# Attention and two gated blocks on one core: no weight conversions in the attention but one block's, DVE adds the 1e-9, the first products of two chunks interleaved, gates ahead of folds

## The chip, the cores and the metric

The kernel runs on one core of one Trainium2 chip. The metric is the device time of one execution in microseconds (us). The kernel before took 961.48 us, the median of three runs (959.97 to 962.03).

## What is computed

An attention with a bias from positions, then two feed-forward blocks, all in float32 (the weights come as 64-bit words that the kernel converts).

```python
scores = q @ k.T / sqrt(64) + bias        # 4 batches, 8 heads, 576 positions, 64 wide
attn = exp(scores - max); attn = attn / (sum(attn) + 1e-09)
x = attn @ v                              # as 2304 tokens x 512
a = x @ w1; b = x @ w2                    # 512 -> 1024
x2 = (a * b @ w3) @ w_out                 # 1024 -> 1024 -> 512
h = x2 @ w_in; solu = h * softmax(h); out = layernorm(solu) * g @ w_out2
```

## The kernel before

Five engines work from in-order queues of their own: TensorE (PE; PEld is its weight load), VectorE (DVE), ScalarE (ACT), GpSimd (POOL) and SyncE (SP), which issues nearly all DMAs. The order of each queue is the order in which the Python code emits instructions; nothing reorders them later. A float32 product is made of three fp32r matmuls (`three`, L79 to L81): high by high, high by low, low by high. A tile is split into a high half by an ACT cast and a low half by a subtraction on DVE or POOL.

**Bias** (up to 74 us) is not touched.

**Attention** (class `Attention`) goes through 16 pairs of heads in slots, `slot(s)`, ten to a pair. A slot emits, in this order: on ACT an addition of 1e-9 to the sums of exponentials of three slots ago (`inverse(0, ...)`, L410), the high halves of transposed blocks (L505), the copy of a finished output out of PSUM (L507) and one exponential (L403); on DVE the bias addition with row maximum (L396), the reciprocal of those sums (L412) and low halves (L519); on POOL the scaling of the exponentials by the reciprocal (L416); on PE a score product (L383, L79 to L81), four transposes (L426) and four value matmuls (L469). Every 13th slot `conv_ab` starts a conversion of half a block of w1 or w2 from 64-bit words: SP loads 256 KB (tile `wraw`), and from the seventh slot on each slot has one step of it, an ACT step (L69) and four DVE steps (L70 to L73, tile `wx`), and then a store of 128 KB to the tile `big`. There are twelve such halves, for the blocks 1 to 3; `first_ab` of this class converts block 0 in the first slots (tile `wab`).

**Gated** (class `Gated`) computes x2. Tokens come in six chunks `c` of 384, the 1024 columns in eight blocks `f`. `stage1(c, f)`, the *first product*, makes the a and b of a chunk and a block in 24 matmuls in one of two PSUM buffers (tile `ab`); `gate` multiplies them (ACT copy L805, DVE product L806) into the tile `a`, which `put_outs` stores to DRAM (`g_d`). The weights of block f (tile `ab0` to `ab7`) are made by conversions that `convert(n)` emits n steps at a time from a queue: a load of 512 KB (tile `raw`), an ACT step (L69), four DVE steps (L70 to L73, tile `cm`), a high half (ACT, L675) and a low half (DVE, L678). `fold(m)` multiplies w3 and w_out into block m of one matrix (24 matmuls of tile `big` by `w`); `folded` evicts it (ACT L733, DVE L734). `stage2`, the *second product*, takes a stored g (`load_g`, split by `split_g` on ACT and POOL, L61 and L62) by a folded block. The chunk's input x is loaded, summed on POOL (L758) and split (ACT L765, POOL or DVE L767).

The first four first products are emitted in the last slots of the attention (`early`, table `EARLY`), the rest in `run`, one per step: `now` is the step's first product, chunk by chunk; folds stand in steps 17 to 24, second products from step 19 on. A gate is emitted at the start of the step after its product. The conversions of the blocks 4 to 7, of w_out and of w3 are in the queue.

**Solu**, the last block (from 732 us), is not touched.

Of the kernel before, what the change touches and what calls it, by code (L numbers as in the profile page):

```python
# [213 lines left out]
class Attention:  # L214
# [10 lines left out]
    def __init__(self, ch, i, bias, x_d, ga):  # L225
        self.ch, self.nc, self.i = ch, ch.nc, i
        self.bias, self.x_d, self.ga = bias, x_d, ga
        self.pairs = [(p, b) for p in range(NPH) for b in range(NB)]
        self.left, self.right, self.top, self.psl, self.psr = (contextlib.ExitStack() for _ in range(5))
        self.W = {}  # L230
        self.BT = {}
        self.SQ = {}
        self.EV, self.OUT = [], []
        self.later = {}
        self.conv, self.fill = [], []
# [7 lines left out]
    def open_right(self):  # L243
        ch = self.ch
        self.ep = ch.pool(self.right, "ae", "right")
        self.idt = self.ep.tile([128, 128], F, name="idt", tag="idt")
        ch.load(self.idt, self.i["ident"])
        self.eps = self.ep.tile([128, 8], F, name="eps", tag="eps")
        ch.nc.gpsimd.memset(self.eps, 1e-9)
        self.eps = self.eps[:, 0:1]  # L250
        self.tp = ch.pool(self.top, "at", "right")
        self.sps = ch.pool(self.psl, "asp", bufs=2, space=PSUM)
        self.tps = ch.pool(self.psr, "atp", "right", bufs=2, space=PSUM)
        self.ops = ch.pool(self.psr, "aop", "right", bufs=1, space=PSUM)
# [103 lines left out]
    def conv_ab(self, u):  # L358

        ch = self.ch  # L360
        n, hf = divmod(u, 2)
        raw = self.qk.tile([128, 512], U, tag="wraw", name="wraw")
        x = self.qk.tile([128, 256], F, tag="wx", name="wx")
        ch.load(raw.rearrange("p (k f) -> p k f", k=2), self.words(n, 2 * hf, 2))
        nop = lambda: None
        out = lambda: ch.load(self.ga.first[:, n, hf * 256 : hf * 256 + 256].bitcast(F), x)
        return [nop] * 7 + ch.f64_steps(raw.rearrange("p (n t) -> p n t", t=2), x) + [out]

# [36 lines left out]
    def inverse(self, step, n, k, ps, e, st):  # L405
        if k % 2 == 0 and k < 8:
            return
        c = 1 + k % 2
        if step == 0:
            self.nc.scalar.activation(st[:, 4 : 4 + c], st[:, 2 : 2 + c], AF.Identity, bias=self.eps, scale=1.0)  # L410
        else:
            self.nc.vector.reciprocal(st[:, 6 : 6 + c], st[:, 4 : 4 + c])  # L412
# [84 lines left out]
    def slot(self, s):  # L497
# [3 lines left out]
        if s - 3 in SQ:  # L501
            self.inverse(0, *SQ[s - 3])
# [9 lines left out]
        if s - 3 in SQ:  # L512
            self.inverse(1, *SQ[s - 3])
            if SQ[s - 3][1] % 2:
                self.normalise(*SQ[s - 4])
            if SQ[s - 3][1] % 2 or SQ[s - 3][1] == 8:
                self.normalise(*SQ[s - 3])
# [15 lines left out]
        if n < NP:  # L533
# [13 lines left out]
            if s % 13 == 0 and s < 156:  # L547
                self.conv = self.conv_ab(4 + s // 13)
            if self.conv:
                self.conv.pop(0)()  # L550
# [6 lines left out]
class Gated:  # L557
# [8 lines left out]
    EARLY = {7: 0, 10: 1, 12: 2, 14: 3}  # L566
    MID = 8
    FIRST = 4
# [23 lines left out]
    def open_mid(self):  # L592
        ch = self.ch
        self.gp = ch.pool(self.left, "gg")
        gb = ch.pool(self.left, "gb")
        for f in range(1, self.FIRST):
            self.place[f] = gb

    def open_right(self):
# [3 lines left out]
        for f in range(self.FIRST, 8):  # L603
            self.place[f] = self.wp
# [126 lines left out]
    def folded(self, m, ps):  # L731
        t = self.WF[m] = self.wp.tile([128, 2, 512], R, name="wf%d" % m, tag="wf%d" % m)
        self.nc.scalar.copy(t[:, 0], ps)  # L733
        self.nc.vector.tensor_tensor(out=t[:, 1], in0=ps, in1=t[:, 0].bitcast(F), op=ALU.subtract)  # L734

# [77 lines left out]
    def split_g(self, c, f):  # L813
        hi, lo = self.G[(c, f)]
        self.ch.split(hi, lo, lo.bitcast(F))
# [95 lines left out]
    def early(self, n):  # L911

        if n == 0:
            self.queue += [(self.cv_ab, f, w) for f in range(self.FIRST, 8) for w in range(2)]
# [9 lines left out]
        for k in {1: (0,), 2: (1,), 8: (2, 3), 10: (4, 5), 12: (6, 7)}.get(n, ()):  # L924
            self.rests.append(self.first_ab(k))
        if n > 2:
            self.convert(2)
# [4 lines left out]
        if n in self.EARLY:  # L932
            self.stage1(0, self.EARLY[n])
            self.next_x(1, self.EARLY[n])
# [5 lines left out]
    def run(self):  # L940
        steps = [(c, f) for c in range(NC) for f in range(8)]
        late = [(self.cv_win, u) for u in range(8)] + [(self.cv_wo2, f) for f in range(8)]
        late += [(self.mean_rows,)] + [(self.out_wo2, f) for f in range(8)]
        self.last = True
        plan, n = {}, 0
        for s in range(2 * len(steps)):
            many = 0 if s < self.LAG else 1 if s < self.LAG + 8 else 2
            plan[s] = steps[n : min(n + many, max(0, s - self.NEAR))]
            n += len(plan[s])
        for s in range(len(self.EARLY), len(steps) + self.NEAR + 1):  # L950
            m = s - self.FLAG
            fold = 0 <= m < 8
            now = steps[s] if s < len(steps) else None
# [8 lines left out]
            for g in plan[s + 1]:  # L962
                self.load_g(*g)
# [4 lines left out]
            self.convert(6 if fold else 2 if plan[s] else 5)  # L968
            if fold:
                self.folded(m, ps)  # L970
# [5 lines left out]
            if now:  # L976
                self.next_x(now[0] + 1, now[1])
# [242 lines left out]
```

## Time and profile before

| | |
|---|---|
| median of three runs | 961.48 us |
| the profiled execution | 955.43 us, of which the span from first to last instruction 953.6 |
| PE busy | 881.3 us (92%) |
| DVE busy | 627.2 us (66%) |
| ACT busy | 498.7 us (52%) |
| POOL busy | 413.3 us (43%) |
| mean granted clock of TensorE | 0.986 |

Busy shares are means over stages that differ much, so the rows below go by stage. Times in the rows are us from the start of the span; a wait is put down to the engine or DMA that ended last. [...]

### The profile page before, as it was taken

Reading aid. Unit: us, or ns where it says so; the run is one execution under the profiler, and the core shown is the slowest. Engines: PE = TensorE matmul, PEld = TensorE weight load, DVE = VectorE, ACT = ScalarE, POOL = GpSimd, SP = SyncE. Lnnn points to the kernel's source line nnn. Section 1 sums busy time; section 2 is a strip of 40 time slices with the busy share of each in tenths; the row PEclk is TensorE's granted clock in tenths of the full one; section 3 lists DMA queues with packets and bytes.
Section 4 is the critical chain, followed back from the end, with each engine's and each line's share of the span. In section 5 each row is a group of like instructions: output and inputs, shape, how many; then the busy total and the mean of one; then the engine's idle time right before and its main releaser. Section 6 shows DMA issues by size and latency. Waiting matters only on the chain.

```text
span 953.6 us, 16700 instructions
## 1 busy us (share of the span) xinstructions
PE 881.3 (92%) x5890; PEld 791.0 (83%) x5890; DVE 627.2 (66%) x1296; ACT 498.7 (52%) x1086; POOL 413.3 (43%) x465
## 2 busy tenths in 40 slices
PE   5776999999989989899899999988999999999998
PEld 4435889998978978898789999988999888888886
DVE  7999999998989987667565286472511644444442
ACT  8995999999989974334332134222322322233222
POOL 3238788887877650111112175495632222022000
PEclk9998999999999999999999999998999999999999
DMA  4897999999899666474451575575333101101000
GB/s 137 251 305 228 220 260 279 221 308 256 226 257 246 148 213 201 138 219 151 138 171 34 163 231 157 187 238 163 106 124 110 45 23 56 55 23 56 23 23 34
DMA packets 96900, 153.18 MB, mean 161 GB/s; under 512 B 16432, under 2 KB 61360, under 8 KB 96816
## 3 DMA queue, kind: packets, MB, share of 16 engines
q1 hardware_dynamic: 96672, 151.81, 53.9%
q8 instruction: 47, 0.77, 0.3%
q14 instruction: 37, 0.30, 0.1%
q10 hardware_dynamic: 144, 0.29, 0.1%
HBM read 81.40 MB, written 41.30 MB: 129 GB/s over the span
## 4 chain that ended last, share of the span: by engine, by line
PE 61%; DMA 9%; DVE 9%; ACT 9%; issue 6%; POOL 4%; SPq 2%; POOLq 0%; ACTq 0%; DVEq 0%
PE ab L81 10%; PE ab L79 10%; PE ab L80 10%; PE o L81 4%; PE o L80 4%; PE o L79 4%; PE x L80 3%; PE x L81 3%; PE op L469 3%; PE x L79 3%; ACT e L403 3%; DMA k<-kr 3%; PE sp L383 3%; ACT eth L505 3%; PE tp L426 2%
## 5 line engine op out<-in xcount | busy, mean ns | idle before, releaser
L79 PE MATMUL ab<-xh,ab 128*128 128x384 f32 x384 | 130.8, 341 | 9.6 <-ACT ab L675 4.5
L81 PE MATMUL ab<-xh,ab 128*128 128x384 f32 x384 | 130.5, 340 | 1.2 <-DVE ab L678 1.2
L80 PE MATMUL ab<-xl,ab 128*128 128x384 f32 x384 | 130.1, 339 | 0.4 <-DVE xl L767 0.4
L416 POOL TENSOR_SCALAR e<-e,st 128x576 f32<-128x576 f32 x128 | 97.1, 768 | 40.2 <-DVE st L412 39.2
L62 POOL TENSOR_TENSOR gl<-gl,gh 128x384 fp32r<-128x384 f32 x48 | 55.4, 1168 | 132.1 <-ACT gh L61 129.8
L519 DVE TENSOR_TENSOR etl<-tp,eth 128x512 fp32r<-128x512 f32 (+1 forms) x160 | 99.5, 630 | 15.8 <-ACT eth L505 12.3
L383 PE MATMUL sp<-k,q 128*128 128x288 f32 x512 | 92.0, 302 | 11.7 <-DVE st L396 3.9
L403 ACT ACTIVATE e<-e,st 128x576 f32<-128x576 f32 x128 | 100.1, 782 | 3.3 <-DVE st L396 3.2
L396 DVE CUSTOM_DVE_ANT_0 e<-sp,bt 128x576 f32<-128x576 f32 x128 | 95.4, 746 | 2.1 <-PE sp L383 1.7
L426 PE MATMUL tp<-idt,e 128*128 128x128 f32 x576 | 89.0, 276 | 8.0 <-DVE etl L519 4.8
L505 ACT CAST eth<-tp 128x512 fp32r<-128x512 f32 (+1 forms) x160 | 84.5, 539 | 16.5 <-PE tp L426 14.4
L383 PEld LDWEIGHTS sp<-k,q 128*128 128x128 f32 x512 | 75.4, 191 | 16.3 <-DVE st L396 6.4
L1029 DVE TENSOR_REDUCE st<-ab 128x1 f32<-128x1024 f32 x18 | 22.0, 1224 | 99.7 <-PE ab L81 99.7
L1049 POOL TENSOR_TENSOR st<-st,half 128x1 f32<-128x1 f32 x18 | 9.9, 549 | 176.2 <-DVE st L1048 176.2
L79 PEld LDWEIGHTS ab<-xh,ab 128*128 128x128 f32 x384 | 73.2, 191 | 11.9 <-ACT ab L675 5.1
L426 PEld LDWEIGHTS tp<-idt,e 128*128 128x128 f32 x576 | 69.2, 141 | 13.4 <-DVE etl L519 3.9
L81 PEld LDWEIGHTS ab<-xh,ab 128*128 128x128 f32 x384 | 73.2, 191 | 1.8 <-DVE ab L678 1.8
L80 PEld LDWEIGHTS ab<-xl,ab 128*128 128x128 f32 x384 | 73.0, 190 | 0.7 <-DVE xl L767 0.7
L80 PE MATMUL x<-gl,wf 128*128 128x384 f32 x192 | 66.6, 347 | 5.9 <-POOL gl L62 5.9
L469 PE MATMUL op<-eth,v 128*128 128x288 f32 x256 | 65.8, 338 | 6.1 <-ACT o L507 6.1
L192 PE MATMUL ps<-mk,cb 128*32 128x264 bf16 (+17 forms) x1056 | 51.4, 331 | 20.8 <-DVE mk L171 10.5
L79 PE MATMUL x<-gh,wf 128*128 128x384 f32 x192 | 65.8, 343 | 1.8 <-ACT gh L61 1.8
(167 smaller groups left out, 2229.3 us busy)
## 6 DMA issues: line engine op xcount, KB each, us to landing
bias_d<-rs SPq DMA_DIRECT2D x36, 295.5 KB, 3.9
qkr<-in_qk SPq DMA_DIRECT2D x16, 608.0 KB, 5.6
k<-kr SPq DMA_DIRECT2D x32, 288.0 KB, 6.4
x_d<-o SPq DMA_DIRECT2D x64, 144.0 KB, 3.9
g_d<-a SPq DMA_DIRECT2D x48, 192.0 KB, 4.0
gl<-g_d SPq DMA_DIRECT2D x48, 192.0 KB, 2.7
k<-kr SPq DMA_DIRECT2D x32, 256.0 KB, 6.7
raw<-in_wo SPq DMA_DIRECT2D x16, 512.0 KB, 4.0
```

Source lines behind the costliest of these rows:

```text
L62: (eng or self.nc.gpsimd).tensor_tensor(out=lo, in0=x, in1=hi.bitcast(F), op=ALU.subtract)
L79: mm(out, a[0], b[0], start=first, stop=False)
L80: mm(out, a[0], b[1], start=False, stop=False)
L81: mm(out, a[1], b[0], start=False, stop=last)
L383: nc.tensor.matmul(ps[:, half, :HS], w["q"][:, h, q * 128 : q * 128 + 128], w["k"][:, h, x, half * HS : half * HS + HS], start=x == 0, sto ...
L396: self.nc.vector.tensor_tensor_reduce(out=halves(e), in0=ps[:, :, :HS], in1=halves(self.BT[(self.pairs[n][0], k)]), scale=-0.125, scalar=3e38,
L403: self.nc.scalar.activation(e, e, AF.Exp, bias=st[:, c : c + 1], scale=-1.0, accum_out=st[:, 2 + c : 3 + c])
L416: self.nc.gpsimd.tensor_scalar(out=e, in0=e, scalar1=st[:, c : c + 1], scalar2=1.0, op0=ALU.mult, op1=ALU.mult)
L426: tr = lambda c, src: nc.tensor.transpose(ps[: src.shape[1], c * 128 : c * 128 + 128], src, self.idt)
L469: nc.tensor.matmul(w["op"][:, half, :HS], lhs, rhs, start=c == 0 and x == 0, stop=c == 4 and x == 1)
L505: self.nc.scalar.copy(hi, src)
L519: self.nc.vector.tensor_tensor(out=lo, in0=src, in1=hi.bitcast(F), op=ALU.subtract)
```

## The change

The additions of 1e-9 move from ACT to DVE, ahead of the reciprocal, with no `eps` tile. `conv_ab` is gone; all blocks but 0 are converted in the queue of Gated, as whole blocks of 512 columns. Of the first products that stand in the attention's last slots one less is emitted by step count (three, of which the last is of chunk 1); in `run` the chunks 0 and 1 go side by side, block by block. Chunk 1's x is loaded early, into tiles that the folded blocks 4 to 7 use later. In a step with a fold, the step's own gate is emitted ahead of the fold's eviction. Odd blocks of g get their low half on DVE. The loads of g go ahead by up to four. `convert` takes more steps where there is no fold.

```diff
 class Attention
-        self.eps = self.ep.tile([128, 8], F, name="eps", tag="eps")
-        ch.nc.gpsimd.memset(self.eps, 1e-9)
-    def conv_ab(self, u):
...
-    def inverse(self, step, n, k, ps, e, st):
+    def inverse(self, n, k, ps, e, st):
         if k % 2 == 0 and k < 8:
             return
         c = 1 + k % 2
-        if step == 0:
-            self.nc.scalar.activation(st[:, 4 : 4 + c], st[:, 2 : 2 + c], AF.Identity, bias=self.eps, scale=1.0)
-        else:
-            self.nc.vector.reciprocal(st[:, 6 : 6 + c], st[:, 4 : 4 + c])
+        self.nc.vector.tensor_scalar(out=st[:, 4 : 4 + c], in0=st[:, 2 : 2 + c], scalar1=1e-9, scalar2=None, op0=ALU.add)
+        self.nc.vector.reciprocal(st[:, 6 : 6 + c], st[:, 4 : 4 + c])
...
-        if s - 3 in SQ:
-            self.inverse(0, *SQ[s - 3])
...
-            if s % 13 == 0 and s < 156:
-                self.conv = self.conv_ab(4 + s // 13)
-            if self.conv:
-                self.conv.pop(0)()
 class Gated
-    EARLY = {7: 0, 10: 1, 12: 2, 14: 3}
+    EARLY = {7: (0, 0), 10: (0, 1), 14: (1, 0)}
     MID = 8
-    FIRST = 4
...
+    def wf(self, m):
+        return self.place[1 if m > 3 else 2].tile([128, 2, 512], R, name="wf%d" % m, tag="wf%d" % m)
...
-        self.ch.split(hi, lo, lo.bitcast(F))
+        self.ch.split(hi, lo, lo.bitcast(F), self.nc.vector if f % 2 else None)
...
-            self.queue += [(self.cv_ab, f, w) for f in range(self.FIRST, 8) for w in range(2)]
+            self.queue += [(self.cv_ab, f, w) for f in range(1, 8) for w in range(2)]
...
-        for k in {1: (0,), 2: (1,), 8: (2, 3), 10: (4, 5), 12: (6, 7)}.get(n, ()):
-            self.rests.append(self.first_ab(k))
+        if 0 < n < 3:
+            self.rests.append(self.first_ab(n - 1))
+        if n == self.MID:
+
+            for k in range(4):
+                t = self.wf(4 + k)
+                self.X[(1, k)] = [t[:, y, :TC] for y in range(2)]
+                self.load_x(1, k, self.X[(1, k)])
+        for k in {10: (0, 1), 12: (2, 3)}.get(n, ()):
+            self.XS[(1, k)] = self.sum_x(1, self.X[(1, k)], self.xp, "xs", 2)
+        for k in {11: (0, 1), 13: (2, 3)}.get(n, ()):
+            self.split_x(1, k, self.XS.pop((1, k)))
         if n > 2:
-            self.convert(2)
+            self.convert(2 if n < 9 else 3)
...
-            self.stage1(0, self.EARLY[n])
-            self.next_x(1, self.EARLY[n])
+            self.stage1(*self.EARLY[n])
...
+        order = sorted(steps, key=lambda g: g if g[0] > 1 else (0, g[1] // 2 if g[1] < 2 else g[1], g))
+        at = {g: s for s, g in enumerate(order)}
...
-            plan[s] = steps[n : min(n + many, max(0, s - self.NEAR))]
+            plan[s] = [g for g in steps[n : n + many] if at[g] < s - self.NEAR]
...
-            now = steps[s] if s < len(steps) else None
+            now = order[s] if s < len(steps) else None
...
-            for g in plan[s + 1]:
-                self.load_g(*g)
+            while loaded < min(used + 4, len(steps)) and at[steps[loaded]] < s - 1:
+                self.load_g(*steps[loaded])
+                loaded += 1
+            used += len(plan[s])
...
-            self.convert(6 if fold else 2 if plan[s] else 5)
+            self.convert(6 if fold else 2 if plan[s] else 7)
             if fold:
+                if now:
+                    self.gate(*now)
                 self.folded(m, ps)
                 self.convert(6)
...
-            if now:
-                self.next_x(now[0] + 1, now[1])
+            if now and s > 7:
+                self.next_x(max(2, now[0] + 1), s % 8)
```

How this moves instructions, at three places. First DVE's queue in the middle of the attention, in two slots of a pair, before (`etl` is a transposed block's low half, `e` the scores with bias, `st` the sums, `wx` the conversion's tile):

```order
L519 TENSOR_TENSOR etl<-tp,eth 128x512
L70 TENSOR_SCALAR wx<-wx 128x256
L396 ISA e,st<-sp,bt 128x576
L396 ISA st 128x1
L412 RECIPROCAL st<-st 128x2
L519 TENSOR_TENSOR etl<-tp,eth 128x512
L71 TENSOR_SCALAR wx<-wx 128x256
```

and in the change:

```order
L501 TENSOR_TENSOR etl<-tp,eth 128x512
L382 ISA e,st<-sp,bt 128x576
L382 ISA st 128x1
L395 TENSOR_SCALAR st<-st 128x2
L396 RECIPROCAL st<-st 128x2
```

The conversion's steps are gone, and the addition L395 stands directly ahead of the reciprocal that needs it.

Second, PE's queue from the second first product on: the first matmul of each of six consecutive first products (the 23 that follow each are left out). The first number is the PSUM tile's, `xh` is chunk 0's input, `wf4` chunk 1's, and `ab1` to `ab6` are the weights of the blocks. Before:

```order
L79 MATMUL ab_6105<-xh_5891,ab1_6075 128x384
L79 MATMUL ab_6146<-xh_5891,ab2_6096 128x384
L79 MATMUL ab_6193<-xh_5891,ab3_6141 128x384
L79 MATMUL ab_6249<-xh_5891,ab4_6238 128x384
L79 MATMUL ab_6298<-xh_5891,ab5_6247 128x384
L79 MATMUL ab_6343<-xh_5891,ab6_6283 128x384
```

and in the change:

```order
L79 MATMUL ab_6016<-xh_5781,ab1_5985 128x384
L79 MATMUL ab_6081<-wf4_5965,ab0_5813 128x384
L79 MATMUL ab_6121<-wf4_5965,ab1_5985 128x384
L79 MATMUL ab_6173<-xh_5781,ab2_6152 128x384
L79 MATMUL ab_6220<-wf4_5965,ab2_6152 128x384
L79 MATMUL ab_6265<-xh_5781,ab3_6161 128x384
```

PE's products stand at the same places of its queue, but of another chunk and block: chunk 1 comes at the third product, and a new block is needed at every second one.

Third, DVE's queue around the second fold (`wf_6977` and `wf_6930` are the second fold's low halves, `a` a gate, `w` the low half of w3). Before:

```order
L71 TENSOR_SCALAR cm<-cm 128x512 x2
L72 SCALAR_TENSOR_TENSOR cm<-raw,cm 128x512 x2
L73 SCALAR_TENSOR_TENSOR cm<-raw,cm 128x512 x2
L734 TENSOR_TENSOR wf_6977<-ab,wf_6977 128x512
L678 TENSOR_TENSOR w_6973<-cm,w_6973 128x512
L70 TENSOR_SCALAR cm<-cm 128x512
L678 TENSOR_TENSOR w_6975<-cm,w_6975 128x512
L70 TENSOR_SCALAR cm<-cm 128x512
L71 TENSOR_SCALAR cm<-cm 128x512 x2
L72 SCALAR_TENSOR_TENSOR cm<-raw,cm 128x512 x2
L806 TENSOR_TENSOR a<-ab,a 128x384
```

and in the change:

```order
L653 TENSOR_TENSOR w_6917<-cm,w_6917 128x512
L653 TENSOR_TENSOR w_6919<-cm,w_6919 128x512
L70 TENSOR_SCALAR cm<-cm 128x512 x2
L71 TENSOR_SCALAR cm<-cm 128x512 x2
L784 TENSOR_TENSOR a<-ab,a 128x384
L709 TENSOR_TENSOR wf_6930<-ab,wf_6930 128x512
```

The gate stood behind the fold's low half and a run of conversion steps; now it stands directly ahead of the fold's low half. ACT's two copies that feed them move in the same way.

## Rows read from the trace of the kernel before

**Rows 1.** By stage: stretch, length, busy PE PEld DVE ACT POOL, clock, DMA, GB/s.

```profile
78.00:336.00 258.00, 238.04 (x1800) 226.01 (x1799) 236.99 (x609) 232.96 (x596) 206.05 (x232) 0.99 0.91 242
336.00:372.00 36.00, 29.94 (x180) 28.06 (x180) 28.58 (x52) 21.27 (x46) 13.48 (x14) 0.95 0.66 208
372.00:441.00 69.00, 62.91 (x337) 61.31 (x338) 48.19 (x93) 28.04 (x53) 11.24 (x10) 0.95 0.60 180
441.00:500.00 59.00, 53.19 (x256) 46.54 (x255) 35.60 (x60) 18.13 (x33) 8.40 (x7) 0.97 0.46 150
500.00:732.00 232.00, 224.35 (x1238) 218.20 (x1238) 106.78 (x134) 66.67 (x140) 114.81 (x100) 0.99 0.47 148
```

**Rows 2.** Waits of PE from 78 to 335 us: total us, times, longest.

```profile
PE op L469 <- ACT o L507: 5.4, 10, 0.8
PE sp L383 <- DVE st L396: 3.5, 5, 1.6
PE sp L383 <- DMA k<-kr: 3.4, 3, 1.5
PE tp L426 <- DVE etl L519: 2.9, 4, 1.9
PE sp L383 <- DVE wx L72: 2.2, 1, 2.2
```

**Rows 3.** Groups of instructions: busy us, mean ns, idle before.

```profile
L410 ACT ACTIVATE st<-st,eps 128x2 f32<-128x2 f32 (+1 forms) x80 | 23.6, 295 | 2.4
...
L412 DVE RECIPROCAL st<-st 128x2 f32<-128x2 f32 (+1 forms) x80 | 12.6, 157 | 3.0 <-ACT st L410 2.8
...
L70 DVE TENSOR_SCALAR wx<-wx 128x256 f32<-128x256 f32 x12 | 8.5, 712 | 0.0
```

**Rows 4.** The tile wx alone, 78 to 336 us: busy DVE, ACT, clock, DMA.

```profile
78.00:336.00 258.00, 29.76 (x48) 5.20 (x12) 0.99 0.91 242
```

**Rows 5.** Timeline around a conversion step: start us, duration us, engine, line.

```profile
108.30 0.75 POOL L416 TENSOR_SCALAR e<-e,st 128x576 f32<-128x576 f32 x1
...
109.01 1.56 POOL L57 TENSOR_TENSOR ql<-qkr,qh 128x640 fp32r<-128x640 f32 x1
...
109.11 1.60 DVE L70 TENSOR_SCALAR wx<-wx 128x256 f32<-128x256 f32 x1
```

**Rows 6.** Waits of POOL, whole span: total us, times, longest.

```profile
POOL e L416 <- DVE st L412: 39.2, 46, 3.6
```

**Rows 7.** Groups of DVE from 372 to 441 us.

```profile
L73 DVE SCALAR_TENSOR_TENSOR cm<-raw,cm 128x512 uint32<-128x512 uint32 x16 | 10.8, 683 | 0.0
...
L70 DVE TENSOR_SCALAR cm<-cm 128x512 f32<-128x512 f32 x14 | 6.7, 476 | 0.0
```

**Rows 8.** Waits of PE from 335 to 740 us.

```profile
PE x L80 <- POOL gl L62: 5.9, 6, 1.7
PE ab L79 <- ACT ab L675: 4.5, 2, 2.9
PE ab L79 <- DVE a L806: 3.8, 2, 2.2
PE ab L79 <- DVE wf L734: 3.6, 3, 1.4
...
PE x L79 <- ACT gh L61: 1.8, 1, 1.8
```

**Rows 9.** Timeline of SP's queue.

```profile
354.49 0.99 SPq L47 DMA_DIRECT2D raw<-in_w  x2
```

**Rows 10.** Instructions on the tile xl from 330 to 480 us: ns least/median/most, then landing.

```profile
L47 SPq DMA_DIRECT2D xl<-x_d x18: 319/430/694, 336.2 to 455.3; - x18
L758 POOL TENSOR_TENSOR xs<-xh,xl x14: 992/1040/1500, 343.7 to 463.0; 128x384 f32<-128x384 f32 x14
...
DMA to landing us min/median/max: 2.1/4.7/7.5
```

**Rows 11.** Timeline of ACT: the gate's copy after the second first product.

```profile
362.22 0.48 ACT L805 COPY a<-ab 128x384 f32<-128x384 f32 x1 [1.39 <-PE ab L81]
```

More of the change, by code (lines that the diff above doesn't have):

```diff
@@ L234, in __init__ @@
         self.later = {}
-        self.conv, self.fill = [], []
+        self.fill = []
     def open_left(self):
@@ L247, in open_right @@
         ch.load(self.idt, self.i["ident"])
-        self.eps = self.ep.tile([128, 8], F, name="eps", tag="eps")
-        ch.nc.gpsimd.memset(self.eps, 1e-9)
-        self.eps = self.eps[:, 0:1]
         self.tp = ch.pool(self.top, "at", "right")
@@ L356, in load_bias @@
             self.bias.read(t[:, :, :64], row, 2 * p + 1, 512)
-    def conv_ab(self, u):
[L360 to L367, printed above, removed]
     def scores(self, n, k):
@@ L512, in slot @@
         if s - 3 in SQ:
-            self.inverse(1, *SQ[s - 3])
+            self.inverse(*SQ[s - 3])
             if SQ[s - 3][1] % 2:
@@ L594, in open_mid @@
         self.gp = ch.pool(self.left, "gg")
-        gb = ch.pool(self.left, "gb")
-        for f in range(1, self.FIRST):
-            self.place[f] = gb
+        self.place[1] = ch.pool(self.left, "gb")
     def open_right(self):
@@ L602, in open_right @@
         self.wp = ch.pool(self.right, "gw", "right")
-        for f in range(self.FIRST, 8):
+        for f in range(2, 8):
             self.place[f] = self.wp
@@ L731, in folded @@
     def folded(self, m, ps):
-        t = self.WF[m] = self.wp.tile([128, 2, 512], R, name="wf%d" % m, tag="wf%d" % m)
+        t = self.WF[m] = self.wf(m)
         self.nc.scalar.copy(t[:, 0], ps)
         self.nc.vector.tensor_tensor(out=t[:, 1], in0=ps, in1=t[:, 0].bitcast(F), op=ALU.subtract)
+    def wf(self, m):
+        return self.place[1 if m > 3 else 2].tile([128, 2, 512], R, name="wf%d" % m, tag="wf%d" % m)
     def spot(self):
@@ L944, in run @@
         self.last = True
-        plan, n = {}, 0
+        plan, n, loaded, used = {}, 0, 0, 0
         for s in range(2 * len(steps)):
             many = 0 if s < self.LAG else 1 if s < self.LAG + 8 else 2
-            plan[s] = steps[n : min(n + many, max(0, s - self.NEAR))]
+            plan[s] = [g for g in steps[n : n + many] if at[g] < s - self.NEAR]
             n += len(plan[s])
```

## The prediction

> **What bounds the kernel now.** I read the busy time stage by stage first [rows 1]. From 78 to 336 us, the attention, TensorE (PE), DVE and ACT are busy 238, 237 and 233 of 258 us, and the 16 DMA engines 91%. No engine bounds that stage alone; three in-order queues at some 91% hold each other up, and PE stands idle for 20 us. From 336 us on, PE is the engine that all others serve: the tail of the attention (336 to 372) has 6.1 us of PE idle, the first products (372 to 441) 6.1, the folds (441 to 500) 5.8, the second products (500 to 732) 7.7. [...] After 732 us nothing is touched. [...]
>
> Which waits make up the 20 us is in [rows 2]: 5.4 us for ACT's copy of an output out of PSUM, 3.5 for the bias addition on DVE, 3.4 for the keys' DMA, 2.9 for the low half of a transposed block, 2.2 for a conversion step on DVE. The first four end at the engine that is late in that slot, so what makes ACT and DVE late is what counts.
>
> **The attention.** Removed from ACT are 80 additions of 1e-9, 23.6 us [rows 3], and 12 first conversion steps, 5.2 us [rows 4]: 28.8 of 233 us. Removed from DVE are 48 conversion steps, 29.8 us [rows 4]. Twelve loads of 256 KB, twelve stores of 128 KB and their places in SP's queue go too. Added to DVE are 80 additions on 128x2 or 128x1 elements. The trace has none of just this form beside a busy POOL. From below, the nearest row is the reciprocal of the same operand, 157 ns [rows 3]: 12.6 us. From above, the nearest is the conversion step L70, a scalar operation on an SBUF tile as well, at 712 ns [rows 3]: 57 us. That one is long because it ends only with a POOL operation that began before it: the step at 109.11 takes 1.60 us beside a POOL operation from 109.01 for 1.56 [rows 5]. The addition stands directly ahead of its reciprocal, and POOL was idle, waiting for that reciprocal, in 46 of 80 cases at least [rows 6]; there nothing can hold it. In the other 34, half of a usual POOL operation (0.75 us [rows 5]) is 0.38 us: 13 us together. I take 12.6 + 13 = 25.5 us, since the reciprocal is the nearer row: the same operand, the same place. DVE then still has 4 us less, ACT 29 us less. [...]
>
> Of PE's waits I let go: all 2.2 for the conversion step, half of the 5.4 and of the 3.5 (the slots where ACT copies an output also held an addition of 1e-9), two thirds of the 2.9 (ACT there stood for a conversion's DMA), a third of the 3.4: 2.2 + 2.7 + 1.8 + 1.9 + 1.1 = 9.7; less 0.7 for the additions. **Attention: -9 us.** Bounds: -15 if nearly all waits go, -4 if only those go that name a conversion.
>
> **The tail and the first products.** The twelve half conversions come back as six whole ones behind the attention, ahead of the first fold. DVE gets 6 x (2 x 0.48 + 3 x 0.68) = 18 us [rows 7] (the step L71 is taken like L70, the step L72 and the low half like L73), less six low halves at 0.68 that it had there already: +14. Its idle time from 336 to 441 is 36.0 - 28.6 + 69.0 - 48.2 = 28 us [rows 1], so the work fits, if it fits in order: with two chunks side by side a block of weights is wanted every second product, not at each. That removes the waits for a fresh block, 4.5 us, and the shorter of the two waits for a gate, 3.8 - 2.2 = 1.6 us [rows 8]; with them go 3 of the 3.4 us of half clock: -9. But the third product now needs chunk 1 early. Its 16 loads stand behind two loads of raw weights that SP issued from 354.49 for 0.99 us [rows 9], and take SP 0.43 us each [rows 10] and a little between them: SP is done at about 363. Such loads landed 2.1 to 7.5 us after their issue, in the middle 4.7 [rows 10]; these are half as large, so I let the last data be there 3 us later, and two sums and two splits on POOL at about 1.04 us [rows 10] follow: about 370.5. PE is ready for that product at 362.2, where the second one ends [rows 11]; its 24 matmuls at 62.9 / 337 = 0.19 us [rows 1] would end at 366.7. Waiting for its last quarter, it ends at about 371.5: +5 us, and +1.5 for the half clock behind the gap. **Tail and first products: -2.5 us.** Bounds: -10 without the new stall, +5 with it and half of the old waits.
>
> **The folds.** The gate of the product ahead of each fold now stands ahead of the fold's own eviction on ACT and DVE, so the next product's PSUM is free when the fold ends. PE's waits for the fold's low half, 3.6 us, and the 2.2 us wait for a gate, the longer of two, which stands ahead of the third fold [rows 8], have no reason left, and most of the 1.8 us of half clock goes: 7.6, of which I take 6 since the fold's eviction then ends 0.5 us (one gate) later. **Folds: -6 us**, bounds -7.5 and -2.
>
> **The second products.** Half of the 48 low halves of g go from POOL to DVE. PE waits 5.9 us for them on POOL and 1.8 for the high half [rows 8]; the first of each pair stays on POOL, but POOL's queue is shorter, so I let half of these 7.7 us go, less 0.4 for DVE being held by POOL. The earlier loads of g cost nothing: POOL and ACT wait for them behind PE. **Second products: -3.5 us**, bounds -7 and 0.
>
> **The sum** is -9 - 2.5 - 6 - 3.5 = -21. The profiled execution took 955.4 us (span 953.6), so that one would be 934.4; it lay 6.1 us under the median of the three runs, 961.5, which is what is measured: 940.5.
>
> **The rivals.**
> 1. The transfers bound the attention. For: 91% DMA busy at 242 GB/s [rows 1], and PE waits for the keys. Against: 4.6 MB of some 62 leave. Then the attention gains only 4, the second products nothing: -4 - 2.5 - 6 = -12.5, 949.
> 2. DVE becomes the bound before the first fold. For: +14 us of work into 28 us of idle time, of which most stands ahead of gates and may not be usable. Then the 14 come through to PE, and the block waits stay: -9 + 14 - 6 - 3.5 = -4.5, 957. Against: the blocks are wanted half as often.
> 3. Slower: each addition of 1e-9 takes what L70 takes. Place: the DVE queue in the attention, where the low halves and the bias additions stand behind it. Price: 57 - 29.8 = +27 us on an engine that is busy 237 us and waits some 11 more for ACT: 275 against 258, +17 us; with the rest, +17 - 2.5 - 6 - 3.5 = +5, 966.5. It decides from a mean of about 0.65 us per addition. For: the rows of L70; against: POOL idle at 46 of 80. [...]
> 4. Better: no stall for chunk 1, most waits of the attention gone: -15 - 8 - 7 - 5 = -35, 926.5.
> That the change does not do what it says is excluded by the order of the instructions.
>
> **How the numbers follow.** Chances: forecast 0.55 (its own range 933 to 948), rival 1 0.17, rival 2 0.13, rival 3 0.10, rival 4 0.05. What a measurement can tell from no change is about 0.2%, 1.9 us. Rivals 1 and 4 and the forecast are faster; of rival 2, 0.07 is faster, 0.03 the same, 0.03 slower; of rival 3, 0.09 is slower and 0.01 the same. So 0.84, 0.04 and 0.12. The range from 928 to 958 leaves out rival 3, a part of rival 2 and half of rival 4, some 0.18.
>
> **What would show it.** In the new profile the first fold should start about 11 us earlier than at 440.9, the scores end about 9 us earlier; the additions on DVE should average 0.2 to 0.3 us; PE should wait for chunk 1 around its third first product, hardly any more behind the folds; and POOL's low halves of g should cost it some 3 us. Additions above 0.6 us, a DVE without idle time ahead of the folds while PE stands still, or a first fold no earlier than now would make the prediction wrong.

## The result and the profile after

The change takes 950.09 us, the median of four runs (947.66 to 951.89), against 960.73 of the kernel before beside it: a ratio of 0.990 (95% interval 0.985 to 0.994). Forecast were 940.5 and a range of 928 to 958: the direction and the range hold, but only half of the 21 us came.

The profiled execution of the change took 950.4 us (span 948.6), that of before 955.4. I divided both spans at four events read from PE's timeline: the start of the first of the first products, the start of the first fold, the end of the eighth fold, and the start of Solu. These are the stretches of before, then of the change; the columns are those of [rows 1].

```profile
78.00:352.10 274.10, 249.58 (x1872) 235.99 (x1872) 248.76 (x631) 245.63 (x623) 216.78 (x243) 0.98 0.90 242
352.10:440.87 88.77, 81.19 (x447) 79.27 (x446) 64.86 (x121) 36.65 (x69) 13.98 (x13) 0.96 0.60 181
440.87:533.08 92.21, 86.40 (x422) 76.62 (x422) 49.02 (x80) 25.72 (x49) 14.49 (x12) 0.98 0.41 129
533.08:731.87 198.79, 191.14 (x1070) 188.12 (x1070) 93.49 (x113) 59.09 (x124) 108.72 (x95) 0.98 0.50 158
```

```profile
78.00:342.25 264.25, 246.04 (x1874) 237.99 (x1875) 245.51 (x666) 227.11 (x532) 214.10 (x243) 0.97 0.88 233
342.25:438.62 96.37, 81.99 (x447) 77.63 (x446) 79.46 (x144) 41.29 (x77) 16.57 (x15) 0.98 0.66 208
438.62:524.78 86.16, 84.65 (x422) 75.48 (x422) 45.29 (x83) 25.48 (x49) 10.64 (x9) 1.00 0.34 112
524.78:726.96 202.18, 193.12 (x1071) 189.24 (x1071) 97.88 (x133) 58.48 (x123) 86.31 (x74) 0.97 0.52 162
```

| stretch | forecast | profiled change |
|---|---|---|
| attention, to the start of the first products | -9 | -9.9 |
| first products, to the first fold | -2.5 | **+7.6** |
| folds | -6 | -6.0 |
| second products | -3.5 | **+3.4** |
| Solu | 0 | -0.1 |
| sum | -21 | -5.0 |

Two terms came out as forecast, two did not. In the first products DVE is busy 79.5 us where it had been 64.9, and PE idles 14.4 us where it had idled 7.6. What PE and ACT wait for in that stretch of the change:

```profile
ACT cm L69 <- DMA raw<-in_wo: 13.7, 8, 3.1
ACT cm L69 <- DMA raw<-in_w: 13.2, 9, 3.5
PE ab L79 <- DVE a L784: 9.1, 4, 4.2
ACT cm L69 <- DMA raw<-in_w3t: 7.4, 5, 2.7
...
ACT a L783 <- DMA g_d<-a: 4.3, 1, 4.3
...
PE ab L80 <- POOL wf L745: 2.2, 2, 1.3
```

The waits for a fresh block (4.5 us in [rows 8]) are gone, as forecast. In their place PE waits 9.1 us for gates, and ACT stands 34.3 us at the first step of conversions (L69), waiting for raw words. One such place, ACT, then SP, DVE and PE (in brackets the idle time of the engine ahead of the instruction, and what ended it):

```profile
381.01 0.70 ACT L69 ACTIVATE cm<-raw 128x512 f32<-128x512 f32 x1 [2.73 <-DMA raw<-in_w]
382.35 0.66 ACT L69 ACTIVATE cm<-raw 128x512 f32<-128x512 f32 x1 [0.63 <-DMA raw<-in_w]
382.91 0.46 ACT L783 COPY a<-ab 128x384 f32<-128x384 f32 x1
...
376.80 0.92 SPq L47 DMA_DIRECT2D raw<-in_w  x2
...
383.41 0.56 DVE L784 TENSOR_TENSOR a<-ab,a 128x384 f32<-128x384 f32 x1 [1.31 <-ACT a L783]
...
384.02 0.45 PE L79 MATMUL ab<-xh,ab 128*128 128x384 f32 x1 [1.11 <-DVE a L784]
```

SP issues two loads of raw words at 376.80. ACT comes to their first steps, waits 2.73 and 0.63 us, and only then copies the gate that stands behind them in its queue; DVE waits 1.31 us for that copy and PE 1.11 for DVE's product.

PE's four waits for gates are 1.1, 1.4, 2.5 and 4.2 us long, and not all stand behind such a step. The first is the one above, and the second is of its kind. At the third, DVE reaches the gate late: its last two operations ahead of it take 1.50 and 1.21 us beside sums of x on POOL, and they began late behind a first step that waited 2.56 us on ACT. The fourth and longest stands behind another thing: ACT's copy waits for a store of g_d, that is for a free buffer of tile `a`. PE and ACT there, and the granted clock of the 3.65 us that follow (0.56: it reads 0.50 from 422.5 to 425.5, where PE's matmuls start every 0.32 us, and 1.00 from 426.0 to 430.0, where they start every 0.17):

```profile
422.35 0.69 PE L79 MATMUL ab<-wf,ab 128*128 128x384 f32 x1 [4.16 <-DVE a L784]
...
421.23 0.48 ACT L783 COPY a<-ab 128x384 f32<-128x384 f32 x1 [4.27 <-DMA g_d<-a]
```

```profile
422.35:426.00 3.65, 3.65 (x12) 3.65 (x13) 3.57 (x6) 2.06 (x4) 0.76 (x1) 0.56 0.38 104
```

The kernel before has the same wait, and it is the shorter of the two waits for a gate in [rows 8]:

```profile
427.61 0.44 PE L79 MATMUL ab<-xh,ab 128*128 128x384 f32 x1 [1.57 <-DVE a L806]
...
426.49 0.48 ACT L805 COPY a<-ab 128x384 f32<-128x384 f32 x1 [4.96 <-DMA g_d<-a]
```

The theory that I tested: **at seven steps per product, a conversion's first step stands too close behind its load, and the gate behind it in ACT's queue pays.** The rivals: DVE simply has too much work (my rival 2), or the interleaving itself does it.

### The profile page after: what moved, and what is told of

Its sections match the earlier page's. It is cut to its first block, busy times and chain, and to the rows that moved or that the text cites. A ratio compares the mean times of both kernels' runs of the same rounds, so it can differ in the third digit from the quotient of the medians.

```text
span 948.6 us, 16734 instructions
## 1 busy us (share of the span) xinstructions
PE 878.4 (93%) x5890; PEld 791.1 (83%) x5890; DVE 639.0 (67%) x1374; ACT 483.4 (51%) x1000; POOL 386.6 (41%) x442
## 4 chain that ended last, share of the span: by engine, by line
PE 64%; DVE 13%; DMA 12%; issue 3%; ACT 3%; SPq 3%; POOL 2%; ACTq 0%; DVEq 0%; POOLq 0%
PE ab L79 9%; PE ab L81 9%; PE ab L80 9%; PE op L453 5%; PE tp L410 5%; PE sp L369 4%; PE o L80 4%; PE o L81 4%; PE o L79 4%; PE x L80 3%; PE x L81 3%; PE x L79 3%; DMA k<-kr 2%; DMA bt<-bias_d 2%; DMA g_d<-a 2%
## 5 line engine op out<-in xcount | busy, mean ns | idle before, releaser
L79 PE MATMUL ab<-xh,ab 128*128 128x384 f32 x320 | 108.5, 339 | 3.9 <-DVE a L784 2.6
L81 PE MATMUL ab<-xh,ab 128*128 128x384 f32 x320 | 107.6, 336 | 0.4 <-DVE ab L653 0.4
L80 PE MATMUL ab<-xl,ab 128*128 128x384 f32 x320 | 107.5, 336 | 0.2 <-DVE xl L745 0.2
L389 ACT ACTIVATE e<-e,st 128x576 f32<-128x576 f32 x128 | 100.2, 783 | 4.1 <-DVE st L382 3.8
L382 DVE CUSTOM_DVE_ANT_0 e<-sp,bt 128x576 f32<-128x576 f32 x128 | 95.8, 748 | 5.9 <-PE sp L369 5.1
L62 POOL TENSOR_TENSOR gl<-gl,gh 128x384 fp32r<-128x384 f32 x24 | 27.7, 1156 | 120.5 <-ACT gh L61 120.4
L79 PE MATMUL x<-gh,wf 128*128 128x384 f32 x192 | 66.4, 346 | 2.9 <-ACT gh L61 2.9
L81 PE MATMUL x<-gh,wf 128*128 128x384 f32 x192 | 66.1, 345 | 0.0
L79 PEld LDWEIGHTS ab<-xh,ab 128*128 128x128 f32 x320 | 60.1, 188 | 6.8 <-DVE a L784 5.1
L169 ACT ACTIVATE mk<-lt,nb,scb 128x512 bf16<-128x512 f32 (+17 forms) x99 | 64.4, 741 | 2.6 <-DVE scb L148 1.5
```

What stands on the lines that cost most here:

```text
L79: mm(out, a[0], b[0], start=first, stop=False)
L80: mm(out, a[0], b[1], start=False, stop=False)
L81: mm(out, a[1], b[0], start=False, stop=last)
L169: self.nc.scalar.activation(m[:, :w], self.lt[:, :w], AF.Sigmoid, bias=self.nb[:, 1:2], scale=self.scb[:, t : t + 1])
L382: self.nc.vector.tensor_tensor_reduce(out=halves(e), in0=ps[:, :, :HS], in1=halves(self.BT[(self.pairs[n][0], k)]), scale=-0.125, scalar=3e38,
L389: self.nc.scalar.activation(e, e, AF.Exp, bias=st[:, c : c + 1], scale=-1.0, accum_out=st[:, 2 + c : 3 + c])
```

## The experiments

Each was timed beside the kernel before (e12 was only profiled), and its profile divided at the same four events. For orientation, the lengths in us of the four stretches (the attention from 0):

| kernel | attention | first products | folds | second products | ratio to before (95%) |
|---|---|---|---|---|---|
| before | 352.1 | 88.8 | 92.2 | 198.8 | |
| before again (e12) | 354.8 | 90.5 | 90.6 | 198.7 | |
| the change | 342.3 | 96.4 | 86.2 | 202.2 | 0.990 (0.985 to 0.994) |
| e1 | 356.6 | 90.0 | 92.3 | 198.1 | 1.002 (1.000 to 1.004) |
| e2 | 354.4 | 100.6 | 95.6 | 200.1 | 1.016 (1.013 to 1.020) |
| e3 | 342.2 | 98.3 | 84.6 | 199.2 | 0.988 (0.985 to 0.991) |
| e4 | 342.3 | 91.1 | 84.2 | 206.0 | 0.985 (0.982 to 0.988) |
| e5 | 343.9 | 96.7 | 87.1 | 199.0 | 0.992 (0.989 to 0.995) |
| e6 | 342.6 | 97.0 | 89.8 | 199.8 | 0.990 (0.988 to 0.993) |
| e7 | 339.6 | 93.8 | 87.0 | 198.1 | 0.986 (0.984 to 0.989) |
| e8 | 342.4 | 86.7 | 85.7 | 201.0 | 0.980 (0.976 to 0.983) |
| e9 | 355.0 | 92.4 | 87.6 | 203.9 | 1.006 (1.003 to 1.008) |
| e10 | 342.3 | 100.2 | 86.7 | 197.9 | 0.991 (0.988 to 0.995) |
| e11 | 339.9 | 85.8 | 85.8 | 201.7 | 0.978 (0.975 to 0.982) |
| e13 | 337.2 | 94.1 | 87.2 | 196.6 | 0.986 (0.983 to 0.990) |
| e14 | 339.5 | 95.8 | 86.2 | 195.5 | 0.984 (0.980 to 0.987) |
| e15 | 343.4 | 85.2 | 85.9 | 202.4 | 0.976 (0.972 to 0.980) |

One profile shows one execution. With the same attention the change's variants start their first product between 339.5 and 342.6. Where the stretch's code is the change's, the first products take 93.8 to 97.0 us, the folds 84.2 to 87.2 and the second products 196.6 to 206.0; with the code of before, second products take 198.1 to 203.9. The profiled executions of e13 and e14 were the fastest of their six.

### Which part of the attention's edit counts

**e1**, the additions alone:

```diff
-        if step == 0:
-            self.nc.scalar.activation(st[:, 4 : 4 + c], st[:, 2 : 2 + c], AF.Identity, bias=self.eps, scale=1.0)
-        else:
+        if step == 1:
+            self.nc.vector.tensor_scalar(out=st[:, 4 : 4 + c], in0=st[:, 2 : 2 + c], scalar1=1e-9, scalar2=None, op0=ALU.add)
```

> The kernel before with one thing changed: the 80 additions of 1e-9 go from ACT to DVE, ahead of the reciprocal; the conversions stay in the attention. Theory: ACT's 23.6 us of additions are a good part of what the attention gained (first product 9.9 us earlier in the change), although DVE gets busier: first product 3 to 6 us earlier than 352.1, the rest as before, 955 to 958 us. Rival: only the conversions' leaving frees the attention, and DVE with additions and conversions is later: first product at 352 or later, 961 us or more.

It gains nothing (961.36 against 959.28): the rival holds. Up to 336 us, PE's waits for ACT's copies of the output fall from 5.4 us to 0.6, and those for DVE's low halves rise from 2.9 to 7.7. **e5** is the inverse, the change with the additions back on ACT.

> The change with the additions of 1e-9 back on ACT (as before, at the start of the slot); the conversions stay out of the attention. Theory now: the attention's gain comes from the conversions that left, and the additions on DVE are worth little alone (the kernel before with them alone had its first product at 356.6); but with DVE freed, ACT would be the next queue that is late: first product 2 to 5 us later than 342.3, time 952 to 955. Rival: DVE is now the late one, and without the additions (18 us busy) the first product comes at 340 or earlier and the time falls to 948 or less.

949.72, the first product 1.6 us later, at 343.9: later, as the theory has it, but by less than its 2 to 5, and no difference in time where it has 952 to 955 (the additions keep DVE busy for 27.5 us in the change, not 18). PE's waits of e5 from 78 to 336, then those of the change:

```profile
PE op L458 <- ACT o L496: 7.2, 11, 0.7
PE sp L372 <- DMA k<-kr: 5.6, 3, 3.7
PE sp L372 <- DVE st L385: 2.9, 3, 1.6
...
PE tp L415 <- DVE etl L508: 1.1, 1, 1.1
```

```profile
PE sp L369 <- DMA k<-kr: 5.7, 3, 2.3
PE sp L369 <- DVE st L382: 3.5, 4, 1.6
PE tp L410 <- DVE etl L501: 3.2, 10, 0.5
...
PE op L453 <- ACT o L489: 0.4, 1, 0.4
```

The additions' move takes 6.8 us of waits off ACT's copies of the output and gives 2.1 back at DVE's low halves, 0.6 at its bias additions and more in small ones. What freed the attention is that the conversions left: with them it takes 352 to 357 us (before, e12, e1, e2), without them 337 to 344. Whether their steps on ACT, those on DVE or their transfers count most is not separated.

**e2** keeps the twelve half conversions in the attention (`conv_ab` as before), with the rest as in the change.

> The change, but the twelve half conversions of the blocks 1 to 3 stay in the attention; only their high and low halves are made in the queue of Gated. Theory: the work that came back behind the attention is what made the stretch from first product to first fold 96.4 us where it had been 88.8: here it should take 84 to 88 us, with the waits for gates (9.1 us) mostly gone, while the attention loses 3 to 6 of its 9.9 us: the sum 4 to 6 us faster than the change, some 945. Rival: the stretch is longer because of the interleaving of two chunks (late x of chunk 1, the place of the gates): then it stays at 93 or more, and the kernel is as slow as the change or slower, 950 to 955.

974.51, and neither: its attention is that of before (354.4), which bears out the last sentence. But the first products take 100.6 us. DVE is busy 74.1 us there instead of 79.5, and yet PE waits 7.1 us for gates, 4.8 of them behind a store of g_d. And PE waits 6.0 us for chunk 1's x at the third product: ACT's cast of that x stands behind a first step that waits 12.2 us for raw words, whose load SP issued behind the sixteen loads of that x. It is the order of the theory, ahead of another urgent instruction.

### What lengthened the first products

**e3** puts every second low half of the converted weights on POOL (`late_rest` alternates `gpsimd` and `vector`).

> The change, with every second low half of the converted weights on POOL, which has little to do there. If DVE's amount of work bounds the stretch ahead of the first fold, it has some 7 us less of it there, and the stretch falls from 96.4 to 90 us or so: 944. If instead the gates come late because ACT stands at a conversion's first step, waiting for a load of raw words (27 us of such waits from 372 to 438), the stretch stays within 2 us of 96.4 and the time at about 950.

947.94, and the stretch did not shrink (98.3); PE waits 8.7 us for gates. It is no clean test of DVE's work, though: DVE lost 12 instructions there and no time (79.3 us). The low halves of e3 in the stretch, and those of the change:

```profile
L655 DVE TENSOR_TENSOR ab<-cm,ab 128x512 fp32r<-128x512 f32 x7 | 8.6, 1241 | 2.2 <-ACT ab L650 2.2
```

```profile
L653 DVE TENSOR_TENSOR ab<-cm,ab 128x512 fp32r<-128x512 f32 x14 | 8.9, 684 | 1.0 <-ACT ab L650 0.9
```

The seven that stayed take 1.24 us each in the mean, the change's fourteen 0.68. That operations of DVE can take longer beside POOL is seen in the change, ahead of PE's third wait for a gate: 1.50 us (L653) and 1.21 (L70), where ones before and behind them take 0.69 and 0.41.

**e4** is one number, how far a first step stands behind its load, in turns (a turn is one step that `convert` emits):

```diff
-                if e["step"] == 1 and self.turn - e["born"] > 9:
+                if e["step"] == 1 and self.turn - e["born"] > 16:
```

> The change, but the first step (ACT) of a conversion that is not yet among the two active ones is emitted only 16 turns behind its load instead of 9. If the gates are late because ACT stands at such a step and waits for the load, ACT waits less there and the stretch from first product to first fold falls by 2 to 5 us from 96.4: 946. If DVE's amount of work bounds it, nothing changes (950) or DVE now waits for the first step and it gets slower by 1 to 3.

944.63 (an interval that meets the change's), and the stretch 91.1: ACT's waits for raw words fall from 34.3 to 1.7 us, PE's for gates from 9.1 to 4.3. The first three of the four, 5.0 us, are all but gone. The fourth stays, 3.8 us, where ACT waits 6.1 us for a store of g_d: two of the three buffers `a` hold sums of x there. **e8** is e4 with those sums in another tile:

```diff
-                self.XS[(c, k)] = self.sum_x(c, X[(c, k)], self.gp, "a", 3)
+                self.XS[(c, k)] = self.sum_x(c, X[(c, k)], self.rp, "cm", 6)
```

> The kernel with the late first conversion step (944.6 us), and the two sums of x that took two of the three buffers of the gates (tile a) put into another tile. If the wait of 3.8 us ahead of the third to last product before the folds, where ACT waits 6.1 us for a store of g_d, comes from these two buffers, it goes, and some of the waits for high halves of g in the second products go too: 938 to 941. Rival: the gate then waits for something else there (the sums wait for a conversion's tile instead), and the time stays at 943 to 946.

939.21, with an interval clear of the change's, and the stretch 86.7. PE's waits for high halves of g in the second products did not go (4.0 us, 2.9 in the change). The waits in the first products:

```profile
PE ab L80 <- POOL wf L745: 2.0, 2, 1.3
PE ab L79 <- ACT w L650: 1.9, 1, 1.9
PE ab L80 <- DVE xl L745: 1.4, 1, 1.4
PE ab L79 <- DVE a L784: 1.4, 1, 1.4
PE ab L79 <- ACT wf L743: 0.7, 1, 0.7
```

So two things had made the gates late, the first steps (5.3 us of the stretch) and the buffers of the gates (4.4 more); e8's edit without e4's was not run. The two chunks are interleaved here as in the change, and the stretch is shorter than before (88.8): the interleaving itself is not the cause.

**e11** is e8 with no conversion step in the attention's slot 7, so that the loads of chunk 1's x precede two loads of raw words on SP.

> The kernel of 939.2 us (late first step, gates' buffers free), with no conversion step in the attention's slot ahead of the loads of chunk 1's x, so that these do not stand behind loads of raw words on SP. PE waits 2.7 us for that x there. If the loads decide, these waits go, with the half clock behind them: 2 to 4 us less, 936. If POOL's four sums and four splits (10 us in a row) decide, the waits stay and the time is 938 to 941.

938.83: by the time no difference, though the waits for that x fell from 2.7 to 1.5 us. Its row settles another question:

```profile
339.89:425.64 85.75, 78.07 (x446) 76.14 (x444) 78.31 (x136) 38.92 (x74) 17.08 (x15) 1.00 0.71 222
```

DVE is busy 78.3 us, as in the change (79.5), in a stretch 10.6 us shorter. So DVE's amount of work was not the bound in the change; the order was. PE's matmuls, too, are busy 78.1 us at a clock of 1.00 here, against 82.0 at 0.98.

**e10** leaves the first step early and lowers the pace: `FLAG` 20, `LAG` 22, five steps instead of seven.

> The change with the folds and second products three steps later (FLAG 20, LAG 22) and five conversion steps per product instead of seven; the first step of a conversion as early as in the change. If it is the pace that makes ACT wait for raw words and the gates late, those waits fall under 20 us and PE's waits for gates under 4 us, while the stretch to the first fold holds three products more (13.3 us): 103 to 106 us instead of 96.4 + 13.3 = 109.7, time 944 to 947. If the gates are late whatever the pace, the stretch is 108 or more and the time 950.

In the stretch as the theory has it, and shorter than the 103 to 106 expected: without the three added products (13.3 us, an estimate) it takes 100.2 - 13.3 = 86.9 us, ACT waits 10.1 us for raw words and PE 3.4 for gates. In the time not (951.33): the second products start later and PE stands 14.7 us at their high halves of g, once for 7.6; the gain is given back.

**e9** makes e4's edit in the kernel before.

> The kernel before with one number changed: the first step (ACT) of a conversion that is not yet active is emitted 16 turns behind its load instead of 9. If the early first step hurts only where conversions run at the pace of the change (ACT waited 34 us for raw words there, 12 here), this gains little: stretch from first product to first fold 86 to 89 us (88.8 before), time within 2 us of the kernel before. Rival: it is a flaw of both kernels, and this gains 4 to 6 us, as in the change: then it was no reason for the failed term.

965.0, slower, and the stretch 92.4, not 86 to 89: there a fresh block is wanted at each product, and the later first step makes it late (9.1 us of such waits instead of 4.5). ACT had waited only 9.9 us for raw words in that stretch. The early first step suits the kernel before and harms at the change's pace.

### The folds, the second products, the additions

**e6** puts the gate back behind the fold's eviction.

> The change with the gate of a step with a fold put back behind the fold's eviction. If the gate's place is what shortened the folds from 92.2 to 86.2 us, they take 90 to 92 us here and the time is 954 to 956. Rival: the folds are shorter because fewer conversions are left for their stretch (they come earlier, at a pace of seven steps): then they stay at 86 to 87 us and the time at 950.

The folds take 89.8 us, between the two expectations, and PE waits again as in [rows 8]:

```profile
PE ab L79 <- DVE wf L709: 4.8, 4, 1.4
```

So the gate's place is worth some 3 us in that stretch (the folds of the other runs take 84.2 to 87.2); the time (949.2) does not show it beside 950.1.

**e7** leaves all low halves of g on POOL, **e14** gives those of the even blocks to DVE instead of the odd ones (`f % 2` turned round).

> The change with all low halves of g on POOL, as before. If their half on DVE is worth what I had forecast, the second products (202.2 us in the change) get 2 to 4 us longer: 953. If PE's waits there come from ACT, whose high halves of g stand behind a gate that waits for the store of an older gate, they stay at 200 to 203 us, and the time within 1.5 us of 950.

> The change with the low halves of the even blocks of g on DVE and those of the odd ones on POOL (in the change the other way round). PE's waits of 6.1 us for low halves are for the first of each pair, which is POOL's in the change. If its length there counts (POOL 1.05 us, DVE 0.55 and more beside POOL), PE waits 2 to 4 us less and the second products take 196 to 198 us (199 to 202 in the runs with the change's order). If the high half on ACT is late, the waits stay within 1.5 us of 9 in all and the stretch at 198 to 202.

944.85 and 946.15: intervals that meet the change's, and e7 has none of the loss of 2 to 4 us that it would have if DVE's half were worth what I had forecast. PE's waits in the second products, of the change, of e7 and of e14, one kernel to a fence; those of before are in [rows 8]:

```profile
PE x L80 <- POOL gl L62: 6.1, 7, 1.4
PE x L79 <- ACT gh L61: 2.9, 2, 1.8
```

```profile
PE x L80 <- POOL gl L62: 6.1, 6, 1.3
PE x L79 <- ACT gh L61: 2.0, 2, 1.8
```

```profile
PE x L80 <- DVE gl L62: 5.3, 4, 2.4
PE x L79 <- ACT gh L61: 1.8, 1, 1.8
```

Whoever makes them, PE waits 5 to 6 us for low halves. One place in the change, ACT, then POOL and PE:

```profile
569.65 0.48 ACT L783 COPY a<-ab 128x384 f32<-128x384 f32 x1 [9.34 <-DMA g_d<-a]
570.02 0.93 ACT L61 CAST gh<-gl 128x384 fp32r<-128x384 f32 x2
...
570.62 1.00 POOL L62 TENSOR_TENSOR gl<-gl,gh 128x384 fp32r<-128x384 f32 x1 [3.62 <-ACT gh L61]
...
570.59 0.44 PE L79 MATMUL x<-gh,wf 128*128 128x384 f32 x1 [1.16 <-ACT gh L61]
571.67 0.44 PE L80 MATMUL x<-gl,wf 128*128 128x384 f32 x1 [0.64 <-POOL gl L62]
```

ACT's gate waits 9.34 us for a buffer `a`, the high half stands behind it, and POOL has been idle for 3.62 us when it comes. Giving half of the low halves to DVE can't help there. Of the change's seven waits for low halves, this and three others (2.6 us together) are of that kind, with POOL idle until a late high half comes; at the other three (3.6 us) POOL is still at other operations, low halves of x and of other tiles, which the change left on it. Whether e14's shorter stretch (195.5) is more than the spread of single profiles stays open.

**e13** writes each two-element addition of 1e-9 as two of one element.

> The change with each addition of 1e-9 over two elements written as two additions over one element (144 instead of 80). In the change, 28 of the 64 two-element additions begin while POOL works, and those take 0.20 to 1.47 us; 13 of the 16 one-element additions begin beside POOL too, and all take 0.15. If it is the two elements that make DVE wait for POOL, all 144 take about 0.15 (22 us instead of 27.5 in all), none over 0.25, and DVE's low halves and bias additions behind them are less late: first product at 340 to 342 (342.3), time 948 to 950. Rival: the one-element additions were short because of where they stand (the last of a pair's nine blocks): then the first of each two is as long as now, up to 1.47 us, and the time is 950 to 952.

946.88 (ratio 0.986, the interval meets the change's), the first product at 337.2. The additions of the change, by form, then those of e13:

```profile
L395 DVE TENSOR_SCALAR st<-st 128x2 f32<-128x2 f32 x64 | 25.1, 392 | 0.0
...
L395 DVE TENSOR_SCALAR st<-st 128x1 f32<-128x1 f32 x16 | 2.4, 150 | 0.1
```

```profile
L396 DVE TENSOR_SCALAR st<-st 128x1 f32<-128x1 f32 x144 | 15.7, 146 | 0.1
```

All 144 take 0.13 to 0.16 us, as the theory had it, and keep DVE busy for 15.7 us instead of 27.5 (the two of a pair overlap). **e15** is e11 with them: 937.90, ratio 0.976, the fastest of all, with an interval that meets e11's. Its first product starts at 343.4: a gain of the attention by these additions is not shown.

> The kernel of 938.8 us (late first step, gates' buffers free, chunk 1's loads ahead of the raw ones) with the one-element additions. If these are worth something, 936 to 938; if not, 938 to 940.

**e12**, the kernel before once more, shows where its runs differ.

> The kernel before, unchanged, for a second profile: the first one took 955.4 us, under the median of 958 to 961. If the runs differ in the attention, its first product starts here later than at 352.1 by as much as the run is longer than 955.4, and the stretches behind it are the same within 1 us; the change's attention then gained more than 9.9 us against a usual run. Rival: the runs differ in the second products (half clock behind gaps).

958.14, 2.7 us above the first profile: the first product comes 2.7 us later, and the stretches behind it add up to the same within 0.1 us (one by one they differ by up to 1.7). Against a run like this one the change's attention gained 12.6 us, not 9.9; that is about half of why the medians differ by 10.6 us and the two first profiles by 5.

## Why the prediction was right and wrong

**The attention, right by the sum, wrong by the shares.** Forecast -9 (bounds -15 and -4), measured -9.9 between the profiles, -12.6 against the second one of before; the last bias addition begins at 325.8 instead of 335.4. But of the waits from which I took 9.7 us, only 4.6 went up to 336 us: ACT's copies fell from 5.4 to 0.4 and the conversion step's 2.2 went, while the bias additions stayed at 3.5, the low halves rose from 2.9 to 3.2 and the keys' DMA from 3.4 to 5.7. PE's whole idle time in the stretch fell by 6.3 us; the rest is PE's busy time, 249.6 to 246.0 with the same matmuls, for which I had no term and no run here gives the cause. That the sum met is luck in part. I also let 2.7 + 1.8 us go because the additions left ACT; e1 and e5 show no gain in time from their move, since DVE gives back most of what ACT gains.

**The additions, right.** Forecast 25.5 us, measured 27.5 (343 ns each), and by the mechanism that was forecast: 28 of the 80 were held by POOL where I took 34, and they cost 14.6 us beyond an undisturbed one where I took 13. Rival 3, which needed 0.65 us each, is out: only those 28 were held, all of them of two elements (below).

**The first products, the step that failed.** Forecast -2.5, measured +7.6, outside my +5. I let the waits for fresh blocks, 4.5 us, go, and they went. For chunk 1's x I added 5 + 1.5; it cost 3.3 us, and the 1.5 for half clock behind it did not come (the granted clock is 1.00 from 353 to 358). Three steps were wrong:

- I wrote that DVE's 14 us of added work "fits, if it fits in order", and checked it against idle time. I had costed only DVE's queue of the six conversions; their loads on SP and their first steps on ACT, ahead of the gates, were in no term. They made PE wait 5.0 us for gates (e4).
- I let the wait of 1.6 us for a gate go with those for blocks. It had stood behind ACT's wait for a store of g_d, which nothing in the change touches, and it came back as 4.2 us (e8).
- I let 3 us of half clock go. With gate waits of 9.1 us in place of 1.6, PE's matmuls are busy 82.0 us instead of 81.2; in e11, without these waits, 78.1. That half clock costs PE what the mean clock of a stretch lacks to 1.00, times its length (3.4 us here, 1.8 in the folds), was my estimate, and no run shows that term by itself. What the traces show is the clock at 0.50 for two times 3.4 us in the first products of before (from 374.0 and 391.0) and for one time 3.4 us in those of the change (from 422.2).

Rival 2 had the place and the sign, with +14 for a cause, the amount of work, that e11 refutes.

**The folds, right by the sum and by the mechanism**, -6.0 for -6 (-4.4 against the second profile of before). PE's idle time there fell from 5.8 to 1.5 us, its busy time from 86.4 to 84.7 with the clock at 1.00 (before, it was at 0.50 for 3.4 us, from 466.1); e6 gives some 3 us to the gate's place.

**The second products, the other step that failed.** "POOL's queue is shorter, so I let half of these 7.7 us go": POOL is busy 86.3 us instead of 108.7, and PE waits 9.0 us instead of 7.7. Four of the seven waits for low halves end with a high half that is late on ACT, once behind a gate that waits for a store, and three with other work of POOL. By e7 the term is worth nothing, and the +3.4 of the profiled run lies within the spread of runs of the same code (196.6 to 206.0); it is not shown to be the change's.

**Rival 1** gives 949, close to what came, but its mechanism is out: the attention gained its full term, not 4.

## What to carry to other kernels

When work is moved to another stretch, follow each of its instructions on every queue it passes: comparing its sum with an engine's idle time misses the one instruction that waits for a load ahead of something urgent. Before a wait is let go, read what the engine named in it was waiting for: here it was a store, not a block of weights. How far a load must run ahead depends on the pace; when the pace is changed, the distance has to be set anew (here one number was worth some 5 us of a stretch, and was harmful in the kernel before). And before an operation is moved to a second engine, ask whether its input is what is late, and what else stands in the second engine's queue.

## What the runs showed of the hardware

In the change, a two-element addition on DVE that begins beside an operation of POOL ends with it, a one-element one does not. Of the 64 two-element additions 28 begin while an operation of POOL runs (a split, L54 or L57); they take 0.20 to 1.47 us, and every one ends 0.02 to 0.03 us behind POOL's. The other 36 take 0.16 to 0.17. Of the 16 one-element additions 13 begin beside POOL, and all take 0.15; in e13 none of the 144 takes over 0.16. DVE and POOL at one place of each kind:

```profile
176.26 0.77 DVE L395 TENSOR_SCALAR st<-st 128x2 f32<-128x2 f32 x1
...
175.57 1.43 POOL L57 TENSOR_TENSOR kr<-qkr,kr 128x576 fp32r<-128x576 f32 x1
```

```profile
172.03 0.15 DVE L395 TENSOR_SCALAR st<-st 128x1 f32<-128x1 f32 x1
...
171.82 0.74 POOL L54 TENSOR_SCALAR qh<-qkr 128x640 fp32r<-128x640 f32 x1
```

The addition at 176.26 ends when POOL's operation does, at 177.0; the one at 172.03 ends in the middle of POOL's. The reciprocal of two elements is not held so: in the kernel before 17 of the 64 (L412) begin beside a split of POOL (L57), and all 17 take 0.15 to 0.17 us; the one at 96.84 takes 0.15 beside a split from 95.86 to 97.29. What makes the addition of two elements wait, and neither that of one nor the reciprocal, is not shown.

And work given to POOL need not come off DVE's time (e3: 12 instructions fewer, 79.3 us for 79.5).
